# Attention scores by symmetry: score tiles left of the diagonal are fetched as transposes of tiles already computed

## The chip, the cores and the metric
The kernel runs on one core of one Trainium2 chip. The metric is the device time of one execution in microseconds, the median over several; the profile is of a single execution of its own. TensorE (PE) multiplies, VectorE (DVE) and ScalarE (ACT) work element by element, and the queue of SyncE (SP) issues all DMAs. All data is fp32; TensorE reads it in the form fp32r.

## The reference
```python
B, S, D = u.shape                                  # 2, 3008, 256; z has 64 columns
scores = (1.0 / S) * np.matmul(z, z.transpose(0, 2, 1))
attn = np.maximum(scores, 0.0) ** 2
x = (u * np.matmul(attn, v)).reshape(B * S, D)     # 6016 tokens
h = x @ w1_in;  x = (h - np.tanh(h)) @ w1_out      # d_ff 2048; the weights come in float64
h = x @ w2_in;  out = (np.maximum(h, 0) + alpha * np.minimum(h, 0)) @ w2_out
```
The scores are z times z transposed: the score of query s and key t is that of query t and key s, within one of the two sequences (batches).

## The kernel before
Every operand of a product is split into a high part (rounded to fp32r) and a low part (what is left), and a product is the sum of two or three matmuls: high by high, low by high, high by low. High parts are copies (L121), on ScalarE or VectorE; low parts are subtractions on VectorE (L124).

The work is cut into blocks of 512 tokens: a sequence of 3008 tokens has six, the last of 448. In the attention a block of queries i (q = 0 to 5 within its sequence) goes over 24 key tiles k of 128 keys; the last has 64 keys, doubled. One step is one key tile of one block. Its front (`front_products`, L296) is two matmuls with the keys as weights (L309): 128 keys by 512 queries of scores in PSUM. ScalarE applies relu and scale (L339), then the square (L342); the result `a` is split, the copy being on VectorE for the first block and for even k, on ScalarE otherwise (L345). The back (`back`, L381) is six matmuls (L396): two halves of v's 256 columns, three products each, added up in PSUM over the 24 steps; the last key tile has four. At a block's end `evacuate` multiplies by u on VectorE (L409) and stores x to DRAM (L410). The two MLPs have 16 steps a block, six front and six back matmuls a step, and more work on ScalarE and VectorE.

The order is written out by hand (`manual_schedule`). `steps` is one list: the attention's 288 steps, of which the last 24 take turns with steps of the first MLP, then both MLPs in turns. At turn t the loop (L504) issues the front of step t + 5 and the back of step t on TensorE; then the pieces deferred by earlier turns (`defer`, L291) and one piece of each load under way (`run_work`, L470); then `evacuate`, the DMAs of weights, and the first activation of step t + 5. What a part defers to turn r is issued r + 1 loops later, by rank. So the high and low parts of a step are issued two to four loops ahead of its back.

SBUF tiles are slots of 128 by 512 taken and dropped by hand from a first-in first-out list (`Slots`, L90): 84 of fp32r operands, 15 of raw data. Loads of z (L140) and v (L202) are asked for some steps ahead; queries are split by `load_queries` (L164), the first block by `load_first` (L169). Weights come in float64 and are taken apart into two fp32 parts by a chain of seven pieces (`split_f64`, L219: five two-source and two one-source instructions on VectorE, two on ScalarE), one piece a step and one weight tile every 7 steps, 16 for each MLP; those of the second are parked in DRAM and fetched again later (L500). The two series start at steps 20 and 142 (L457).

Of the kernel before, what the change touches and what calls it, by code (L numbers as in the profile page):

```python
# [17 lines left out]
P = 128  # L18
# [4 lines left out]
N_SLOTS = 84  # L23
# [14 lines left out]
def attention_two_mlps_kernel(  # L38
# [25 lines left out]

    nc = tc.nc
# [23 lines left out]

    class Slots:  # L90
# [20 lines left out]
    take, at, drop = mm.take, mm.at, mm.drop  # L111

# [3 lines left out]
    def split(h_key, l_key, src, n, on_vector=False, then=None):  # L116


        def high():
            copy = nc.vector.tensor_copy if on_vector else nc.scalar.copy  # L120
            copy(out=take(h_key)[:, :n], in_=src)  # L121

        def low():
            nc.vector.tensor_sub(out=take(l_key)[:, :n], in0=src, in1=f32(at(h_key)[:, :n]))  # L124
            if then:
                then()

        return [high, low]

# [34 lines left out]
    def load_queries(b, c):  # L164
        key = "zhh", b, c
        st, n = load_zt(key, b, c)
        return split(key, ("zll", b, c), st[:, :n], n, then=lambda: raw.drop(("st",) + key))

    def load_first():  # L169

        hl, hh, ll = ((z, 0, 0) for z in ("zhl", "zhh", "zll"))
        st, n = load_zt(hl, 0, 0)

        def low(c0, c1):
            nc.vector.tensor_sub(out=at(hl)[DQK:, c0:c1], in0=st[DQK:, c0:c1], in1=f32(at(hh)[DQK:, c0:c1]))  # L175

        def do():
            nc.vector.tensor_copy(out=take(hh), in_=st)  # L178
            nc.scalar.copy(out=take(hl)[:DQK], in_=st[:DQK])  # L179
            low(0, P)  # L180
            nc.vector.tensor_sub(out=take(ll), in0=st, in1=f32(at(hh)))
            low(P, n)
            raw.drop(("st",) + hl)

        return [do]
# [100 lines left out]

    banks = {}
    accs = {}
    turns = deque([] for _ in range(4))
# [6 lines left out]
    def front_products(kind, i, k):  # L296
        n = blocks[i][2]
# [24 lines left out]
    def front_activation(kind, i, k):  # L322

        n = blocks[i][2]
        ps = banks.pop((kind, i, k))
        key = kind, i, k

# [9 lines left out]
        if kind == 0:  # L337
# [42 lines left out]

    def back(kind, i, k):  # L381
# [4 lines left out]
        last = k == (KF if kind else KT) - 1  # L386
        if k == 0:
            accs[kind] = acc_pairs.popleft()
        acc = accs[kind]
        todo = [(wh, h), (wl, h), (wh, l)]  # L390
        if kind == 0 and last:
            todo = [(wh, h), (wh, l)]
        for d in range(KD):
            for e, (w, x) in enumerate(todo):
                c0 = o * D + d * P
                nc.tensor.matmul(out=acc[d][:, :n], lhsT=at(w)[:, c0:c0 + P], rhs=at(x)[:, :n],  # L396
                                 start=k == 0 and e == 0, stop=last and e == len(todo) - 1)
# [28 lines left out]
    streams = [[(0, i, k) for i in range(NBLK) for k in range(KT)]]  # L426
# [30 lines left out]
    for m, w_in, w_out, s0 in ((2, w2_in, w2_out, 20), (1, w1_in, w1_out, 142)):  # L457
# [43 lines left out]

    with tc.manual_schedule():
        warm_up()
        for t in range(-2 * LOOKAHEAD - LEAD, len(steps)):  # L504
# [17 lines left out]
            if t >= 0 and kind == 0 and k == KT // 2:  # L522
                load_u(i)
# [36 lines left out]
```

## Time and profile before
| | us |
|---|---|
| median of 3 runs (1548.41 to 1548.7) | 1548.49 |
| profiled execution, its time | 1548.68 |
| its span, first to last instruction | 1546.7 |
| busy: TensorE, ScalarE, VectorE | 1541.4, 1311.8, 1258.0 |
| TensorE on L396 and L309, modelled | 1002.0, 752.6 |
| DMA moved | 71.67 MB |

The attention takes the span up to about 567 us, its last 24 steps together with the first steps of the first MLP; the rest are the MLPs. Busy time of TensorE is modelled and pipelined: two matmuls overlap, so single durations (0.385 us) are longer than the pitch at which they follow each other. The granted clock is 1.00 over the span but for its first microseconds.

### The profile page before, as it was taken

Reading aid. Unit: us, or ns where it says so; the run is one execution under the profiler, and the core shown is the slowest. Engines: PE = TensorE matmul, PEld = TensorE weight load, DVE = VectorE, ACT = ScalarE, POOL = GpSimd, SP = SyncE. Lnnn points to the kernel's source line nnn. Section 1 sums busy time; section 2 is a strip of 40 time slices with the busy share of each in tenths; the row PEclk is TensorE's granted clock in tenths of the full one; section 3 lists DMA queues with packets and bytes.
Section 4 is the critical chain, followed back from the end, with each engine's and each line's share of the span. In section 5 each row is a group of like instructions: output and inputs, shape, how many; then the busy total and the mean of one; then the engine's idle time right before and its main releaser. Section 6 shows DMA issues by size and latency. Waiting matters only on the chain.

```text
span 1546.7 us, 19804 instructions
## 1 busy us (share of the span) xinstructions
PE 1541.4 (100%) x6895; PEld 1295.1 (84%) x6895; DVE 1258.0 (81%) x2164; ACT 1311.8 (85%) x2431; POOL 0.2 (0%) x4
## 2 busy tenths in 40 slices
PE   9999999999999999999999999999999999999999
PEld 7888889888888888888888888888888888888888
DVE  8888897777877898888787888888887888888764
ACT  8889998888888998888887888888888878888865
POOL 0000000000000000000000000000000000000000
PEclk9999999999999999999999999999999999999999
DMA  6234442122212230000000000000000000000000
GB/s 170 89 124 136 156 157 91 61 78 75 76 61 84 74 114 26 1 28 1 26 1 5 23 1 28 1 28 1 26 1 28 1 1 26 1 14 1 14 1 26
DMA packets 40660, 71.67 MB, mean 46 GB/s; under 512 B 6128, under 2 KB 14832, under 8 KB 40560
## 3 DMA queue, kind: packets, MB, share of 16 engines
q1 hardware_dynamic: 40560, 70.41, 14.2%
q8 instruction: 54, 0.88, 0.2%
q14 instruction: 46, 0.38, 0.1%
HBM read 49.68 MB, written 20.71 MB: 46 GB/s over the span
## 4 chain that ended last, share of the span: by engine, by line
PE 99%; DMA 0%; DVE 0%; SPq 0%; ACT 0%; issue 0%; DVEq 0%; ACTq 0%
PE acc L396 58%; PE front L309 42%; DMA raw<-in_zT 0%; SPq L140 0%; ACT raw L415 0%; DVE mm L178 0%; DVE mm L175 0%; DVEq L178 0%; ACTq L415 0%
## 5 line engine op out<-in xcount | busy, mean ns | idle before, releaser
L396 PE MATMUL acc<-mm,mm 128*128 128x512 f32 (+1 forms) x4008 | 1002.0, 385 | 0.0
L396 PEld LDWEIGHTS acc<-mm,mm 128*128 128x128 f32 x4008 | 752.6, 188 | 141.2
L309 PE MATMUL front<-mm,mm 128*128 128x512 f32 (+1 forms) x2880 | 752.6, 386 | 0.4 <-DVE mm L175 0.4
L309 PEld LDWEIGHTS front<-mm,mm 128*128 128x128 f32 x2880 | 541.6, 188 | 103.8 <-ACT mm L179 1.3
L124 DVE TENSOR_TENSOR mm<-raw,mm 128x512 fp32r<-128x512 f32 (+1 forms) x731 | 468.7, 676 | 3.7 <-PE acc L396 0.5
L121 DVE CAST mm<-raw 128x512 fp32r<-128x512 f32 (+1 forms) x360 | 151.6, 421 | 94.7 <-ACT raw L342 76.0
L121 ACT CAST mm<-raw 128x512 fp32r<-128x512 f32 (+1 forms) x371 | 223.2, 602 | 0.3 <-DVE raw L374 0.3
L360 DVE TENSOR_TENSOR raw<-front,raw 128x512 f32<-128x512 f32 (+1 forms) x192 | 130.5, 679 | 113.6 <-ACT raw L354 112.9
L350 ACT ACTIVATE raw<-front 128x512 f32<-128x512 f32 (+1 forms) x192 | 113.7, 592 | 121.0 <-PE front L309 120.9
L339 ACT ACTIVATE raw<-front 128x512 f32<-128x512 f32 (+1 forms) x288 | 168.9, 586 | 44.8 <-PE front L309 41.0
L342 ACT ACTIVATE raw<-raw 128x512 f32<-128x512 f32 (+1 forms) x288 | 179.8, 624 | 5.3
L374 DVE SCALAR_TENSOR_TENSOR raw<-raw,nalpha,raw 128x512 f32<-128x512 f32 (+1 forms) x192 | 141.4, 737 | 36.3 <-ACT raw L371 36.1
L363 DVE COPY_PREDICATED raw<-raw,raw 128x512 f32<-128x512 int32 (+1 forms) x192 | 142.9, 744 | 5.7
L357 DVE TENSOR_TENSOR raw<-front,raw 128x512 f32<-128x512 f32 (+1 forms) x192 | 129.7, 675 | 17.5 <-ACT raw L351 17.4
L370 ACT ACTIVATE raw<-front 128x512 f32<-128x512 f32 (+1 forms) x192 | 112.1, 584 | 19.4 <-PE front L309 18.2
L353 ACT ACTIVATE raw<-raw 128x512 f32<-128x512 f32 (+1 forms) x192 | 120.2, 626 | 6.1
L354 ACT ACTIVATE raw<-raw 128x512 f32<-128x512 f32 (+1 forms) x192 | 120.1, 626 | 6.1
L352 ACT ACTIVATE raw<-raw 128x512 f32<-128x512 f32 (+1 forms) x192 | 120.5, 628 | 0.0
L351 ACT ACTIVATE raw<-front 128x512 f32<-128x512 f32 (+1 forms) x192 | 112.9, 588 | 0.0
L371 ACT ACTIVATE raw<-front 128x512 f32<-128x512 f32 (+1 forms) x192 | 111.7, 582 | 0.0
L415 ACT COPY raw<-acc 128x512 f32<-128x512 f32 (+1 forms) x48 | 27.7, 580 | 27.2 <-PE acc L396 25.3
L238 DVE SCALAR_TENSOR_TENSOR raw<-st,raw 128x512 uint32<-128x512 uint32 x32 | 22.1, 690 | 2.1 <-ACT raw L232 1.0
(29 smaller groups left out, 222.5 us busy)
## 6 DMA issues: line engine op xcount, KB each, us to landing
st<-in_moe_w_in SPq DMA_DIRECT2D x16, 512.0 KB, 4.5
st<-in_moe_w_out SPq DMA_DIRECT2D x16, 512.0 KB, 3.8
raw<-in_v SPq DMA_DIRECT2D x22, 256.0 KB, 4.1
raw<-in_uT SPq DMA_DIRECT2D x20, 256.0 KB, 3.1
xd<-raw SPq DMA_DIRECT2D x20, 256.0 KB, 2.3
st<-xd SPq DMA_DIRECT2D x10, 512.0 KB, 3.7
outT<-raw SPq DMA_DIRECT2D x20, 256.0 KB, 2.0
raw<-in_zT SPq DMA_DIRECT2D x38, 128.0 KB, 4.0
```

The lines of the kernel that those rows point to most:

```text
L121: copy(out=take(h_key)[:, :n], in_=src)
L124: nc.vector.tensor_sub(out=take(l_key)[:, :n], in0=src, in1=f32(at(h_key)[:, :n]))
L309: nc.tensor.matmul(out=ps, lhsT=at(w)[:, o:o + P], rhs=at(x)[:, :n], start=e == 0, stop=e == len(todo) - 1)
L339: nc.scalar.activation(out=r, in_=ps, func=AF.Relu, scale=scale)
L342: nc.scalar.activation(out=a, in_=r, func=AF.Square)
L352: nc.scalar.activation(out=g, in_=g, func=AF.Arctan, scale=SMALL_C)
L353: nc.scalar.activation(out=g, in_=g, func=AF.Square, scale=SMALL_A)
L357: nc.vector.tensor_sub(out=t, in0=ps, in1=t)
L360: nc.vector.tensor_mul(out=g, in0=ps, in1=g)
L363: nc.vector.copy_predicated(out=t, mask=mask.bitcast(I32), data=g)
L374: nc.vector.scalar_tensor_tensor(out=r, in0=q, scalar=nalpha_sb[:, k:k + 1], in1=r, op0=ALU.mult, op1=ALU.add)
L396: nc.tensor.matmul(out=acc[d][:, :n], lhsT=at(w)[:, c0:c0 + P], rhs=at(x)[:, :n], start=k == 0 and e == 0, stop=last and e == len(todo) - 1)
```

## The change
In a block q of queries, the score tiles whose keys lie in a block kb < q (4q of 24) are no longer computed. They are the transposes of tiles of the earlier block kb of the same sequence, whose keys lay in block q. There, the squared tile `a` goes through one VectorE instruction that transposes it in 32 by 32 blocks into one of two buffers of four tiles; when the four tiles of a key block are there, SP writes them to DRAM in four DMAs, one for each 32 partitions, in rows of 128 elements (512 bytes). 12 steps ahead of its use SP loads the tile from DRAM into a slot; ScalarE copies the high part, and VectorE subtracts in place.

So that the 32 by 32 blocks come to lie right, the queries of a block stand in another column order (`in_columns`; `in_tokens` is the old one): the copies of the query loads, the multiplication by u and the first load use both views. The order of key tiles in a block changes for q > 0: first those of later blocks, then its own, evenly mixed with the fetched ones. High parts of tiles that are sent on are on ScalarE except every second in a block q = 0; those on the diagonal are on VectorE. The operand slots are 76 instead of 84 up to the attention's last block, when the two buffers are given back as 8 slots; keys and v are dropped as they are used up. The weight series start at steps 30 and 156.
```diff
-N_SLOTS = 84
+Q = 32
+FLIP_BUFS = 2
+FLIP_LEAD = 12
+N_SLOTS = 76
...
+    flip_pool = ExitStack()
+    flip_p = flip_pool.enter_context(tc.tile_pool(name="flip", bufs=1))
+    flip_bufs = [flip_p.tile([P, 4 * NB], F32, name=f"flip{i}") for i in range(FLIP_BUFS)]
...
+    def runs(n):
+
+        t = NB // P
+        if n == NB:
+            return [(0, 0, P // Q, t)]
+        half = HALF // Q
+        return [(0, 0, half, t), (half * t * Q, half, P // Q - half, t - 1)]
+
+    def in_columns(ap, n):
+
+        return [ap[:, c:c + na * nt * Q].rearrange("p (a t r) -> p t a r", a=na, t=nt) for c, _, na, nt in runs(n)]
+
+    def in_tokens(ap, n):
+
+        whole = ap.rearrange("p (t a r) -> p t a r", a=P // Q, r=Q)
+        return [whole[:, :nt, a:a + na] for _, a, na, nt in runs(n)]
...
+
+        def high():
+            for dst, src in zip(in_columns(take(key), n), in_tokens(st, n)):
+                nc.scalar.copy(out=dst, in_=src)
+
+        def low():
+            for dst, src, h in zip(in_columns(take(("zll", b, c)), n), in_tokens(st, n), in_columns(at(key), n)):
+                nc.vector.tensor_sub(out=dst, in0=src, in1=f32(h))
+            raw.drop(("st",) + key)
+
+        return [high, low]
...
         def do():
-            nc.vector.tensor_copy(out=take(hh), in_=st)
+            nc.vector.tensor_copy(out=in_columns(take(hh), n)[0], in_=in_tokens(st, n)[0])
             nc.scalar.copy(out=take(hl)[:DQK], in_=st[:DQK])
-            low(0, P)
-            nc.vector.tensor_sub(out=take(ll), in0=st, in1=f32(at(hh)))
-            low(P, n)
+            low(0, 1)
+            nc.vector.tensor_sub(out=in_columns(take(ll), n)[0], in0=in_tokens(st, n)[0],
+                                 in1=f32(in_columns(at(hh), n)[0]))
+            low(1, NB // P)
...
+    def key_tiles(q):
+
+        c = NB // P
+        if q == 0:
+            return list(range(KT))
+        mine = [k for kb in [*range(q + 1, QB), q] for k in range(kb * c, kb * c + c)]
+        theirs = list(range(q * c))
+        places = [((e + 0.5) / len(ks), k) for ks in (mine, theirs) for e, k in enumerate(ks)]
+        return [k for _, k in sorted(places)]
+
+    tiles_of = [key_tiles(q) for q in range(QB)]
+
+    def is_flipped(i, k):
+        return k * P // NB < i % QB
...
+        if kind == 0 and is_flipped(i, k):
+            return
...
-            if k == KT - 1:
+            if k == [k for k in tiles_of[q] if not is_flipped(i, k)][-1]:
                 drop(("zhh", b, q), ("zll", b, q))
-                if q == QB - 1:
-                    drop(*(("zhl", b, c) for c in range(QB)))
+                if q:
+                    drop(("zhl", b, q))
+                if q == 1:
+                    drop(("zhl", b, 0))
...
-        ps = banks.pop((kind, i, k))
         key = kind, i, k
+        if kind == 0 and is_flipped(i, k):
+            h, l = ("h",) + key, ("l",) + key
+
+            def high():
+                nc.scalar.copy(out=take(h)[:, :n], in_=f32(at(l)[:, :n]))
+
+            def low():
+                nc.vector.tensor_sub(out=at(l)[:, :n], in0=f32(at(l)[:, :n]), in1=f32(at(h)[:, :n]))
+
+            defer((0, 0, high), (1, 3, low))
+            return
+        ps = banks.pop(key)
...
-            on_vector = i == 0 or k % 2 == 0
-            high, low = parts(a, "a", on_vector)
+            b, q = blocks[i][0], i % QB
+            kb, t = divmod(k, NB // P)
+            flip = kb > q
+            on_vector = not flip or q == 0 and k % 2 == 0
+            high, low = split(("h",) + key, ("l",) + key, a, n, on_vector, then=None if flip else lambda: free("a"))
             defer((0, 0, square), (1, 0, high), (1 if on_vector else 2, 3, low))
+
+            def transpose():
+                if t == 0:
+                    flip_bufs.append(flip_bufs.pop(0))
+                buf = flip_bufs[-1]
+                nc.vector.transpose(out=buf.rearrange("p (t a s r) -> p a t s r", t=NB // P, a=P // Q, r=Q)[:, :, :, t],
+                                    in_=a.rearrange("p (a t r) -> p a t r", a=P // Q, r=Q))
+                free("a")
+                if t < NB // P - 1:
+                    return
+                m = blocks[b * QB + kb][2]
+                flips[b, q, kb] = to = dram.tile([NB, m], F32, name=f"flip_{b}_{q}_{kb}")
+                for c, a0, na, nt in runs(m):
+                    for e in range(na):
+                        p0 = (a0 + e) * Q
+                        nc.sync.dma_start(
+                            out=to.rearrange("(f r) c -> r f c", r=Q)[:, :, c + e * nt * Q:c + (e + 1) * nt * Q],
+                            in_=buf[p0:p0 + Q].rearrange("p (f c) -> p f c", c=P)[:, :, :nt * Q])
+
+            if flip:
...
+    def ends(kind, i, k):
+
+        ks = range(KF) if kind else tiles_of[i % QB]
+        return k == ks[0], k == ks[-1]
...
+        first, last = ends(kind, i, k)
+        if first:
             accs[kind] = acc_pairs.popleft()
         acc = accs[kind]
         todo = [(wh, h), (wl, h), (wh, l)]
-        if kind == 0 and last:
+        if kind == 0 and k == KT - 1:
...
-        if k % 2 and i == (NBLK if kind else QB * (b + 1)) - 1:
-            drop(wh, wl)
+        if i == (NBLK if kind else QB * (b + 1)) - 1:
+            used.add((kind, b, k))
+            if (kind, b, k ^ 1) in used:
+                drop(wh, wl)
...
-                x = raw.at(("u", i, d))[:, :n]
-                nc.vector.tensor_mul(out=x, in0=acc[d][:, :n], in1=x)
-                nc.sync.dma_start(out=x_dram[i][:, d, :n], in_=x)
+                x = raw.at(("u", i, d))
+                for there, here in zip(in_columns(acc[d], n), in_tokens(x, n)):
+                    nc.vector.tensor_mul(out=here, in0=there, in1=here)
+                nc.sync.dma_start(out=x_dram[i][:, d, :n], in_=x[:, :n])
...
-    streams = [[(0, i, k) for i in range(NBLK) for k in range(KT)]]
+    streams = [[(0, i, k) for i in range(NBLK) for k in tiles_of[i % QB]]]
...
-    for m, w_in, w_out, s0 in ((2, w2_in, w2_out, 20), (1, w1_in, w1_out, 142)):
+    for m, w_in, w_out, s0 in ((2, w2_in, w2_out, 30), (1, w1_in, w1_out, 156)):
...
+    flipped = deque((t, *step[1:]) for t, step in enumerate(steps) if step[0] == 0 and is_flipped(*step[1:]))
+
+    def run_flipped(t):
+        while flipped and flipped[0][0] <= t + FLIP_LEAD:
+            _, i, k = flipped.popleft()
+            b, _, n = blocks[i]
+            kb, e = divmod(k, NB // P)
+            nc.sync.dma_start(out=f32(take(("l", 0, i, k))[:, :n]), in_=flips[b, kb, i % QB][e * P:(e + 1) * P])
...
-            if t >= 0 and k == (KF if kind else KT) - 1:
+            if t >= 0 and ends(kind, i, k)[1]:
                 evacuate(kind, i)
+            if t == n_att - KF * 3 // 2:
+                flip_pool.close()
+                more = ctx.enter_context(tc.tile_pool(name="more", bufs=1))
+                mm.free.extend(range(N_SLOTS, N_SLOTS + 4 * FLIP_BUFS))
+                mm.tiles += [more.tile([P, NB], F32R, name=f"mm{N_SLOTS + e}") for e in range(4 * FLIP_BUFS)]
+            run_flipped(t)
...
-            if t >= 0 and kind == 0 and k == KT // 2:
+            if t >= 0 and kind == 0 and k == tiles_of[i % QB][KT // 2]:
```

## Rows read from the trace of the kernel before
**Rows 1.** The page's head: span, busy time, granted clock in 40 slices.
```profile
span 1546.7 us, 19804 instructions
PE 1541.4 (100%) x6895; PEld 1295.1 (84%) x6895; DVE 1258.0 (81%) x2164; ACT 1311.8 (85%) x2431; POOL 0.2 (0%) x4
...
PEclk9999999999999999999999999999999999999999
```
**Rows 2.** The chain of waits that ended last, on the page, by line.
```profile
PE acc L396 58%; PE front L309 42%; DMA raw<-in_zT 0%; SPq L140 0%; ACT raw L415 0%; DVE mm L178 0%; DVE mm L175 0%; DVEq L178 0%; ACTq L415 0%
```
**Rows 3.** List of waits: us in total, times, longest.
```profile
DVE mm L121 <- ACT raw L342: 76.0, 88, 1.9
```
**Rows 4.** Timeline of TensorE: start, us, engine, line, operation.
```profile
441.55 0.62 PE L309 MATMUL front<-mm,mm 128*128 128x512 f32 x2
442.00 1.52 PE L396 MATMUL acc<-mm,mm 128*128 128x512 f32 x6
```
**Rows 5.** Timeline of SP's queue: three of the stores of x.
```profile
225.50 1.30 SPq L410 DMA_DIRECT2D xd<-raw  x2
...
264.26 0.87 SPq L410 DMA_DIRECT2D xd<-raw  x2
...
307.38 0.92 SPq L410 DMA_DIRECT2D xd<-raw  x2
```
**Rows 6.** Windows, one per block: engines' busy us (instructions), clock, DMA share, GB/s.
```profile
10.00:53.00 43.00, 43.00 (x191) 35.37 (x190) 39.37 (x75) 39.84 (x73) 0.00 (x0) 1.00 0.40 107
53.00:96.00 43.00, 43.00 (x191) 35.61 (x190) 34.51 (x65) 37.90 (x69) 0.00 (x0) 1.00 0.34 116
96.00:139.00 43.00, 43.00 (x191) 35.64 (x190) 35.35 (x66) 38.50 (x71) 0.00 (x0) 1.00 0.45 141
139.00:182.00 43.00, 43.00 (x192) 35.61 (x191) 37.03 (x68) 39.31 (x73) 0.00 (x0) 1.00 0.42 135
182.00:225.00 43.00, 43.00 (x192) 35.78 (x191) 38.89 (x72) 41.13 (x78) 0.00 (x0) 1.00 0.58 177
225.00:264.00 39.00, 39.00 (x192) 35.87 (x192) 30.28 (x60) 35.43 (x71) 0.00 (x0) 1.00 0.28 93
264.00:307.00 43.00, 43.00 (x191) 35.58 (x191) 34.40 (x64) 38.05 (x69) 0.00 (x0) 1.00 0.21 66
307.00:350.00 43.00, 43.00 (x192) 35.61 (x191) 34.34 (x64) 37.60 (x68) 0.00 (x0) 1.00 0.26 80
...
436.00:479.00 43.00, 43.00 (x192) 35.67 (x191) 30.28 (x56) 36.55 (x68) 0.00 (x0) 1.00 0.16 54
479.00:567.00 88.00, 88.00 (x405) 75.73 (x404) 79.83 (x139) 83.72 (x157) 0.00 (x0) 1.00 0.29 90
```
**Rows 7.** Timeline of VectorE, where it is saturated.
```profile
22.54 0.42 DVE L121 CAST mm<-raw 128x512 fp32r<-128x512 f32 x1
22.99 0.69 DVE L124 TENSOR_TENSOR mm<-raw,mm 128x512 fp32r<-128x512 f32 x1
23.60 0.42 DVE L121 CAST mm<-raw 128x512 fp32r<-128x512 f32 x1
23.95 1.30 DVE L124 TENSOR_TENSOR mm<-raw,mm 128x512 fp32r<-128x512 f32 x2
25.16 0.42 DVE L121 CAST mm<-raw 128x512 fp32r<-128x512 f32 x1
```
**Rows 8.** VectorE's groups: busy us, mean ns; the second from 53 to 479 us.
```profile
L363 DVE COPY_PREDICATED raw<-raw,raw 128x512 f32<-128x512 int32 (+1 forms) x192 | 142.9, 744 | 5.7
...
L234 DVE TENSOR_SCALAR raw<-st 128x512 uint32<-128x512 uint32 x31 | 13.1, 422 | 0.0
```
**Rows 9.** DMA: packets by size, the queue, and x's store with its landing.
```profile
DMA packets 40660, 71.67 MB, mean 46 GB/s; under 512 B 6128, under 2 KB 14832, under 8 KB 40560
...
q1 hardware_dynamic: 40560, 70.41, 14.2%
...
xd<-raw SPq DMA_DIRECT2D x20, 256.0 KB, 2.3
```

More of the change, by code (lines that the diff above doesn't have):

```diff
@@ L166, in load_queries @@
         st, n = load_zt(key, b, c)
-        return split(key, ("zll", b, c), st[:, :n], n, then=lambda: raw.drop(("st",) + key))
+        def high():
[6 more added lines that the diff above has]
+        return [high, low]
     def load_first():
@@ L172, in load_first, with low @@
         st, n = load_zt(hl, 0, 0)
-        def low(c0, c1):
-            nc.vector.tensor_sub(out=at(hl)[DQK:, c0:c1], in0=st[DQK:, c0:c1], in1=f32(at(hh)[DQK:, c0:c1]))
+        def low(t0, t1):
+            nc.vector.tensor_sub(out=in_tokens(at(hl), n)[0][DQK:, t0:t1], in0=in_tokens(st, n)[0][DQK:, t0:t1],
+                                 in1=f32(in_columns(at(hh), n)[0][DQK:, t0:t1]))
         def do():
-            nc.vector.tensor_copy(out=take(hh), in_=st)
+            nc.vector.tensor_copy(out=in_columns(take(hh), n)[0], in_=in_tokens(st, n)[0])
             nc.scalar.copy(out=take(hl)[:DQK], in_=st[:DQK])
-            low(0, P)
-            nc.vector.tensor_sub(out=take(ll), in0=st, in1=f32(at(hh)))
-            low(P, n)
+            low(0, 1)
+            nc.vector.tensor_sub(out=in_columns(take(ll), n)[0], in0=in_tokens(st, n)[0],
+                                 in1=f32(in_columns(at(hh), n)[0]))
+            low(1, NB // P)
             raw.drop(("st",) + hl)
@@ L285, in load_x @@
                 for piece in split(("xh", 1, i, d), ("xl", 1, i, d), st[:, d, :n], n, on_vector=d == 1)]
+    def key_tiles(q):
[9 more added lines that the diff above has]
+        return k * P // NB < i % QB
     banks = {}
     accs = {}
+    flips = {}
+    used = set()
     turns = deque([] for _ in range(4))
@@ L343, in square @@
                 free("r")
-            on_vector = i == 0 or k % 2 == 0
-            high, low = parts(a, "a", on_vector)
-            defer((0, 0, square), (1, 0, high), (1 if on_vector else 2, 3, low))
+            b, q = blocks[i][0], i % QB
[3 more added lines that the diff above has]
+            high, low = split(("h",) + key, ("l",) + key, a, n, on_vector, then=None if flip else lambda: free("a"))
+            defer((0, 0, square), (1, 0, high), (1 if on_vector else 2, 3, low))
+            def transpose():
[16 more added lines that the diff above has]
+            if flip:
+                defer((2, 4, transpose))
         elif kind == 1:
@@ L385, in back @@
         wh, wl = (("vh", b, j), ("vl", b, j)) if kind == 0 else (("woh", kind, j), ("wol", kind, j))
-        last = k == (KF if kind else KT) - 1
-        if k == 0:
+        first, last = ends(kind, i, k)
+        if first:
             accs[kind] = acc_pairs.popleft()
@@ L396, in back @@
                 nc.tensor.matmul(out=acc[d][:, :n], lhsT=at(w)[:, c0:c0 + P], rhs=at(x)[:, :n],
-                                 start=k == 0 and e == 0, stop=last and e == len(todo) - 1)
+                                 start=first and e == 0, stop=last and e == len(todo) - 1)
         drop(h, l)
-        if k % 2 and i == (NBLK if kind else QB * (b + 1)) - 1:
-            drop(wh, wl)
+        if i == (NBLK if kind else QB * (b + 1)) - 1:
+            used.add((kind, b, k))
+            if (kind, b, k ^ 1) in used:
+                drop(wh, wl)
     def evacuate(kind, i):
```

## Prediction
> **What bounds the kernel now.** I read the page's head first. [...] A busy TensorE alone proves nothing, since matmuls are pipelined, so the chain of waits came next: 99% of it are the two matmul lines, L396 and L309, and no other engine holds it for as much as 0.5% [rows 2]. The list of waits has the same answer from the other side: the engines wait for each other, VectorE's casts 76.0 us for ScalarE's square [rows 3], while TensorE waits for nobody after the first microseconds. So a matmul that goes is worth its whole pitch, as long as the other engines follow.
>
> What a matmul costs in the attention stage: an L309 pair starts at 441.55 and the six of L396 behind it at 442.00 [rows 4], so two matmuls take 0.45 us. More exactly from whole blocks: the issues of x's store come 43.12 us apart for a block of 512 queries and 38.76 us for one of 448 [rows 5]. A block has 24 x 8 - 2 = 190 matmuls, which gives 0.2269 and 0.2040 us each.
>
> VectorE is the engine to watch. In a block of the attention it is busy 34.3 to 38.9 of 43 us, ScalarE 36.6 to 41.1 [rows 6]. ScalarE is the busier one; the change relieves it and loads VectorE.
>
> **Removed matmuls.** A block q (0 to 5 in its batch) takes 4q of its 24 score tiles as transposes: 60 a batch, 120 in all. Each saves the two matmuls of L309. The 448-wide block q = 5 has 20 of the 60, so 80 tiles x 2 x 0.2269 = 36.3 us and 40 tiles x 2 x 0.2040 = 16.3 us: **52.6 us** off TensorE's path. The output products (L396) stay as many, and the two MLPs are untouched.
>
> **ScalarE.** 120 tiles lose relu and square and gain one copy (their high part), and in the sending tiles the high part moves to ScalarE. Fewer instructions in every block but the first of each batch, where up to 10 casts are added to an engine that was busy 39.8 of 43 us with more loads around it [rows 6]. No cost.
>
> **VectorE.** Its price of an instruction is not its duration but its pitch when it is saturated, and the stretch from 22 to 25 us shows that: a two-source subtraction of 0.69 us is followed after 0.61 us, two of them after 1.21; a cast (0.42 us) after 0.35, or after 0.45 where its own subtraction waits for it [rows 7].
> The transpose is nowhere in this trace. Bounds: below, the pitch of a one-source SBUF-to-SBUF instruction at VectorE's double pace, 0.34 (a duration of 0.42 less the overlap of 0.08; 0.422 in [rows 8]); above, 0.75, the slowest 512-wide instruction (0.744 us) with no overlap at all [rows 8]. Its output does not stand in the order of its input, which no double-pace row here has, so I take it nearer to the two-source instructions, 0.61 and a little for the strided output: 0.64.
> [...]
>
> Now block by block, VectorE's busy time of [rows 6] with three corrections: casts that go or move (before, all 24 tiles of the first block and 12 of every other; after, 14 in a block q = 0 and 4 in the others, so -8 x 0.45 = -3.6 us in most), transposes (20, 16, 12, 8, 4, 0 by block, at 0.64), and the weight staging, which starts later (steps 30 and 156 instead of 20 and 142). Staging is five instructions at 0.61 and two at 0.34 for every 7 steps, 0.53 us a step [rows 7, 8]. Against it stands the block's time on TensorE, 43.1 us less 0.454 us for each tile saved (0.408 at 448).
> Batch 0: q0 39.4 - 2.1 - 4.6 + 12.8 = 45.5 against 43 (over by 2.5); q1 34.5 - 3.6 + 10.2 - 3.2 = 37.9 against 41.3; q2 35.4 - 3.6 + 7.7 = 39.5 against 39.5; q3 37.0 - 3.6 + 5.1 = 38.5 against 37.7 (over 0.8); q4 38.9 - 3.6 + 2.6 = 37.9 against 35.8 (over 2.1); q5 30.3 - 3.4 + 5.3 = 32.2 against 30.6 (over 1.6).
> Batch 1: q0 34.4 + 0.9 + 12.8 - 6.4 = 41.7 against 43.1; q1 34.3 - 3.6 + 10.2 = 40.9 against 41.3; q2 and q3, from windows within 0.1 us of that, 38.5 and 35.9 against 39.5 and 37.7; q4 30.3 - 3.6 + 2.6 + 5.3 = 34.6 against 35.8; the last block with the MLP's first steps 79.8 - 3.2 + 2.1 = 78.7 against 79.8.
> So VectorE needs 92 to 106% of the shortened blocks. The overs add up to **7.0 us**. Some of that is absorbed: at 22 to 25 us VectorE is saturated [rows 7] while TensorE is busy without a gap [rows 6], since a tile is prepared two to five steps before it is used. But an engine near 100% also loses time to waits that the sums don't show. I let the two cancel and charge 7.0; the ends are 0 (transposes at 0.34 take 36 us off VectorE, and only the last two blocks of batch 0 are over, by 2.5 us together, which the lead can absorb) and about 22 (at 0.75, 120 x 0.11 = 13 us more, nearly all of it in blocks that are full, and 2 of waits).
>
> **DMA and SP.** Each group of four transposed tiles (1.05 MB, 30 groups) is written by four DMAs in pieces of 512 B, 2048 a group, and 120 loads of 224 or 256 KB bring the tiles back. SP issues two DMAs in 0.92 us [rows 5]: 240 more cost about 110 us of a queue that has some 440. What waits behind them on SP are loads and stores with 8 to 14 steps of lead. A tile is fetched 12 steps ahead, at least 16 us; 256 KB land in 2.3 us [rows 9]. Its group was written in an earlier block of the same batch. Hidden.
> A group's buffer is filled again after the next group: in a block q = 0 that leaves 5 steps, 9.1 us, for four writes, and one group each 8.6 us to sustain. If the write is later, the next transpose waits on VectorE with every subtraction behind it, and TensorE for those. The write's price per packet isn't in the trace. From below, by bytes: q1 moved 70.41 MB in 14.2% of 16 x 1546.7 us, 320 GB/s, so 3.3 us a group. From above, the mean packet at any size: 3514 us / 40560 = 87 ns, so 11.1 us a group [rows 9]. Few packets there are below 1 KB other than tiny ones, so neither end is shown; I take about 4 us, hidden, since the transfer by bytes lies nearer to rows of large tiles as these are.
>
> **The rest.** The first query load is copied in another order: 0 to 0.25 us on the start (a cast at 0.69 instead of 0.44); I take 0.2. The slots fall from 84 to 76 until the attention's last block. Their scarcity would show as ScalarE or VectorE waiting for L396, and a slot is written four steps before it is read; nothing is charged, up to 4 us is kept for the range.
>
> **Sum.** The profiled execution took 1548.7 us, 2.0 around its span of 1546.7; the median of the runs is 1548.5, so no correction. 1548.5 - 52.6 + 7.0 + 0.2 = **1503 us**.
>
> **Rivals.**
> *VectorE sets the pace* (1509 to 1530). For it: 92 to 106% leaves no room for a transpose at 0.75 or for one wait of 0.1 us a step. Against it: the waits of VectorE for ScalarE [rows 3] shrink with the casts. Price 22 us or more: about 1518.
> [...]
> *A packet costs the same at any size: slower.* Place: the transpose's wait for its buffer, in the blocks q0 to q2. A group of X us in a queue already taken by 40, 34 and 45% in batch 0 and 21 to 26% in batch 1 [rows 6] needs X/(1 - share), against 8.6, 10.3 and 13.1 us a group. The excess eats the 52.6 us at X near 8.2, 64 ns a packet, which lies between the ends. At X = 9 it loses 76 us: about 1573. Against it: 512 B would then move at 8 GB/s per engine where the mean is 20. [...]
> That the change doesn't remove what it says can be left out: the skipped tiles issue no L309 matmul.
>
> **Chances.** Forecast (1496 to 1508) 0.54; VectorE's pace 0.23; half paths 0.11; packets 0.08 slower; between the last two, no change, 0.04. Faster 0.88, same (within 0.2%, 3 us, what a measurement can tell) 0.04, slower 0.08. The range 1494 to 1528 holds the forecast, most of VectorE's pace and of the half paths; about 0.18 is outside.
>
> **What would show it.** L309 falls from 2880 to 2640 matmuls. Right: block periods from 43 down to about 36 us in batch 0, TensorE's idle below 8 us, the chain still above 97% TensorE, the transpose's mean near 0.7 us. Wrong: L396 waiting for VectorE's subtractions for over 15 us (pace), the transposes waiting for DMA (buffers), or L396 waiting for ScalarE's copies of fetched tiles (the round trip). [...]

## The result: 1510.1 us, and the profile after

| | before | after |
|---|---|---|
| median, us (4 runs each, side by side) | 1548.45 (1548.37 to 1548.7) | 1510.13 (1509.3 to 1512.08) |
| span of the profiled execution | 1546.7 | 1508.5 |
| busy: TensorE, ScalarE, VectorE | 1541.4, 1311.8, 1258.0 | 1494.3, 1231.0, 1288.7 |
| DMA moved, MB | 71.67 | 131.97 |

The ratio is 0.9754, 95% interval 0.9737 to 0.9771. The kernel is faster by 38.3 us, 7 less than forecast: of the 52.6 us of matmuls removed, 14.4 came back as something else (by spans, 1546.7 - 52.6 = 1494.1 against 1508.5).

The chain of waits of the kernel after, by engine and by line, answers to [rows 2]:
```profile
PE 92%; DMA 4%; DVE 2%; ACT 1%; SPq 1%; issue 1%; DVEq 0%; ACTq 0%
```
TensorE holds 92% of it, not 99%: DMA, VectorE, ScalarE and SP now hold some stretches. The list of waits (who waits for whom: us in total, times, longest) has TensorE and the two new lines in it, and below it stands what SP's queue waits for at the writes:
```profile
PEld acc L499 <- DVE mm L137: 8.4, 10, 3.0
ACT mm L393 <- DMA mm<-flip: 6.7, 5, 2.0
PE acc L499 <- DVE mm L137: 4.3, 5, 2.6
DVE flip L430 <- DMA flip<-flip: 2.2, 2, 2.0
...
SPq L440 <- DVE flip L430: 73.1, 22, 8.6
```
No wait is large by itself. TensorE waits for VectorE's subtractions (L137), ScalarE for fetched tiles (L393), VectorE once for a buffer (L430), and SP stands 73 us at the writes (L440) until the transposes are done.

The windows of the six blocks of batch 0 answer to the first six of [rows 6] (busy us of TensorE, its weight loads, VectorE, ScalarE, GpSimd; granted clock; DMA share; GB/s):
```profile
10.00:57.50 47.50, 44.90 (x186) 35.37 (x185) 44.39 (x80) 42.36 (x81) 0.00 (x0) 0.96 0.71 193
57.50:97.80 40.30, 40.30 (x179) 33.36 (x179) 36.02 (x65) 36.22 (x67) 0.00 (x0) 1.00 0.82 236
97.80:138.10 40.30, 40.30 (x180) 33.36 (x179) 39.48 (x70) 35.26 (x63) 0.00 (x0) 1.00 0.91 279
138.10:176.70 38.60, 38.60 (x172) 31.97 (x171) 37.45 (x68) 31.43 (x56) 0.00 (x0) 1.00 0.92 296
176.70:218.00 41.30, 39.60 (x172) 31.15 (x170) 40.84 (x74) 28.27 (x54) 0.00 (x0) 1.00 0.98 314
218.00:249.00 31.00, 29.40 (x136) 24.91 (x137) 29.30 (x57) 20.69 (x41) 0.00 (x0) 1.00 0.74 248
```
VectorE is busy for 89 to 99% of each, and DMA, which was at 28 to 58%, is at 71 to 98%. A modelled TensorE without a gap in the second to fourth windows does not say by itself that it lost nothing there: it is pipelined (0.386 us a matmul, where the next follows after 0.227), and the length of the block has to be looked at.

The loss is placed by the blocks' ends on TensorE: the start of the last of a block's matmuls at L499 (before: L396), read from the trace. The end without loss is that of before less 0.454 us (0.408 at 448) for each saved tile whose front would have been issued up to there (before: 52.71, 263.61 and 585.18 us). The first block's end lies in these four matmuls, before and after:
```profile
52.03 1.07 PE L396 MATMUL acc<-mm,mm 128*128 128x512 f32 x4
```
```profile
56.87 1.08 PE L499 MATMUL acc<-mm,mm 128*128 128x512 f32 x4
```

| end of | without loss, us | after | lost since the row above |
|---|---|---|---|
| the first block | 52.26 | 57.56 | 5.3 |
| batch 0 | 237.29 | 249.39 | 6.8 |
| batch 1 | 532.54 | 547.03 | 2.4 |

The MLPs lose nothing. Block by block the loss is all in a few places: 5.3 in the first block, 2.0 and 4.7 in the last two of batch 0, 2.4 where batch 1 ends beside the first MLP. The second to fourth blocks take 40.80, 38.99 and 37.63 us, which is 43.07 less 5, 9 and 12 tiles at 0.454: they lose nothing, with VectorE busy for 89 to 98% and DMA for 82 to 92%. VectorE's multiplication by u does not mark the end as well: it comes 0.3 us later in the kernel after, and up to 3 us later in kernels below, where VectorE lags and TensorE does not wait for it. The rest of this text uses the same three sums for other kernels: "loses a + b + c".

The first block has the one large stall. VectorE's timeline (start, us; in brackets the idle time ahead and who ended it), then TensorE's, then windows of the stall (columns as above):
```profile
46.37 0.70 DVE L430 STREAM_TRANSPOSE flip<-raw 128x512 f32<-128x512 f32 x1
49.10 0.71 DVE L430 STREAM_TRANSPOSE flip<-raw 128x512 f32<-128x512 f32 x1 [2.03 <-DMA flip<-flip]
```
```profile
47.39 1.98 PE L499 MATMUL acc<-mm,mm 128*128 128x512 f32 x8
51.96 1.96 PE L499 MATMUL acc<-mm,mm 128*128 128x512 f32 x4 [2.59 <-DVE mm L137]
```
```profile
46.00:49.50 3.50, 3.37 (x15) 2.48 (x14) 1.47 (x3) 3.47 (x8) 0.00 (x0) 1.00 1.00 267
49.50:51.90 2.40, 0.00 (x0) 0.00 (x0) 2.33 (x6) 1.60 (x3) 0.00 (x0) 1.00 0.92 268
51.90:55.40 3.50, 3.44 (x8) 2.70 (x9) 3.50 (x7) 0.60 (x1) 0.00 (x0) 0.53 0.99 307
```
A transpose waits 2.03 us for its buffer, all subtractions stand behind it, TensorE idles 2.59 us, and then its granted clock is lower for some 3.4 us (0.53 in the third window, 0.50 in each microsecond from 53 to 55), which do the work of 1.7. So this wait cost about 4.3 of the block's 5.3 us in this execution.

Why the buffer is late shows in SP's queue at 24 to 46 us (start, duration of the issues, line); the buffer is the one whose write was issued from 40.09 on and landed at 48.91:
```profile
24.77 3.07 SPq L440 DMA_DIRECT2D flip<-flip  x4
27.94 2.12 SPq L244 DMA_DIRECT2D raw<-in_v  x2
...
32.27 3.29 SPq L440 DMA_DIRECT2D flip<-flip  x4
...
40.09 5.35 SPq L440 DMA_DIRECT2D flip<-flip  x4
45.48 1.18 SPq L615 DMA_DIRECT2D mm<-flip  x1
```
Four writes are issued in 3.1 to 5.4 us where two stores of x took 0.92 [rows 5], and loads of v stand behind a write that waits: the pair issued at 27.94 was issued at 17.68 before.

### The profile page after: what moved, and what is told of

It is laid out like the page before. It is cut to its first block, busy times and chain, and to the rows that moved or that the text cites. A ratio compares the mean times of both kernels' runs of the same rounds, so it can differ in the third digit from the quotient of the medians.

```text
span 1508.5 us, 19589 instructions
## 1 busy us (share of the span) xinstructions
PE 1494.3 (99%) x6655; PEld 1248.2 (83%) x6655; DVE 1288.7 (85%) x2202; ACT 1231.0 (82%) x2281; POOL 0.2 (0%) x4
## 2 busy tenths in 40 slices
DMA packets 121301, 131.97 MB, mean 87 GB/s; under 512 B 20208, under 2 KB 85232, under 8 KB 121200
## 3 DMA queue, kind: packets, MB, share of 16 engines
q1 hardware_dynamic: 121200, 130.72, 28.2%
## 4 chain that ended last, share of the span: by engine, by line
PE 92%; DMA 4%; DVE 2%; ACT 1%; SPq 1%; issue 1%; DVEq 0%; ACTq 0%
PE acc L499 54%; PE front L370 38%; DMA mm<-flip 1%; DVE mm L137 1%; DMA raw<-in_v 1%; DMA raw<-in_zT 1%; DMA st<-in_moe_w_out 0%; SPq L440 0%; ACT raw L413 0%; DMA w_woh<-mm 0%; DMA w_wil<-mm 0%; DVE mm L396 0%; DVE flip L430 0%; ACT raw L416 0%; SPq L615 0%
## 5 line engine op out<-in xcount | busy, mean ns | idle before, releaser
L499 PE MATMUL acc<-mm,mm 128*128 128x512 f32 (+1 forms) x4008 | 988.9, 386 | 7.5 <-DVE mm L137 4.3
L499 PEld LDWEIGHTS acc<-mm,mm 128*128 128x128 f32 x4008 | 751.6, 188 | 156.5 <-DVE mm L137 8.4
L370 PE MATMUL front<-mm,mm 128*128 128x512 f32 (+1 forms) x2640 | 679.6, 386 | 1.8 <-DVE mm L188 0.9
L370 PEld LDWEIGHTS front<-mm,mm 128*128 128x128 f32 x2640 | 495.6, 188 | 97.2 <-DVE mm L188 1.6
L137 DVE TENSOR_TENSOR mm<-raw,mm 128x512 fp32r<-128x512 f32 (+1 forms) x600 | 389.7, 675 | 4.3 <-ACT mm L134 1.7
L448 ACT ACTIVATE raw<-front 128x512 f32<-128x512 f32 (+1 forms) x192 | 113.4, 591 | 128.7 <-PE front L370 128.6
L134 ACT CAST mm<-raw 128x512 fp32r<-128x512 f32 (+1 forms) x328 | 198.4, 606 | 1.3 <-DVE raw L472 0.3
L413 ACT ACTIVATE raw<-front 128x512 f32<-128x512 f32 (+1 forms) x168 | 99.4, 592 | 45.4 <-PE front L370 44.2
L134 DVE CAST mm<-raw 128x512 fp32r<-128x512 f32 (+1 forms) x272 | 113.6, 418 | 25.6 <-ACT raw L416 7.0
L468 ACT ACTIVATE raw<-front 128x512 f32<-128x512 f32 (+1 forms) x192 | 112.1, 584 | 19.4 <-PE front L370 18.3
L452 ACT ACTIVATE raw<-raw 128x512 f32<-128x512 f32 (+1 forms) x192 | 119.8, 624 | 6.1
L451 ACT ACTIVATE raw<-raw 128x512 f32<-128x512 f32 (+1 forms) x192 | 119.7, 623 | 6.1
L450 ACT ACTIVATE raw<-raw 128x512 f32<-128x512 f32 (+1 forms) x192 | 120.3, 627 | 0.0
L449 ACT ACTIVATE raw<-front 128x512 f32<-128x512 f32 (+1 forms) x192 | 112.8, 588 | 0.0
L469 ACT ACTIVATE raw<-front 128x512 f32<-128x512 f32 (+1 forms) x192 | 111.5, 581 | 0.0
L416 ACT ACTIVATE raw<-raw 128x512 f32<-128x512 f32 (+1 forms) x168 | 106.1, 632 | 3.5
L430 DVE STREAM_TRANSPOSE flip<-raw 128x512 f32<-128x512 f32 x120 | 83.3, 700 | 2.2 <-DMA flip<-flip 2.2
L393 ACT CAST mm<-mm 128x512 fp32r<-128x512 f32 (+1 forms) x120 | 70.4, 595 | 12.5 <-DMA mm<-flip 6.7
```

What stands on the lines that cost most here:

```text
L370: nc.tensor.matmul(out=ps, lhsT=at(w)[:, o:o + P], rhs=at(x)[:, :n], start=e == 0, stop=e == len(todo) - 1)
L448: nc.scalar.activation(out=g, in_=ps, func=AF.Tanh, scale=SMALL_B)
L450: nc.scalar.activation(out=g, in_=g, func=AF.Arctan, scale=SMALL_C)
L451: nc.scalar.activation(out=g, in_=g, func=AF.Square, scale=SMALL_A)
L452: nc.scalar.activation(out=mask, in_=g, func=AF.Relu, scale=-1.0, bias=SMALL_F)
```

## Experiments

All were timed in three rounds. The first four ran beside each other, as did the next four, the next three, and the last by itself; before took 1548.8 to 1549.0 beside them. Two theories for the 14.4 us: VectorE has no room (pace), or the writes and fetches come late (DMA and SP's queue).

**small_writes.** Each write is cut to a sixteenth, and all fetches read one fixed tile; VectorE has all its work.
```diff
-out=to.rearrange("(f r) c -> r f c", r=Q)[:, :, c + e * nt * Q:c + (e + 1) * nt * Q],
+out=to.rearrange("(f r) c -> r f c", r=Q)[:, :1, c + e * nt * Q:c + (e + 1) * nt * Q],
...
-in_=flips[b, kb, i % QB][e * P:(e + 1) * P])
+in_=other[:, :n])
```


> Of each group of transposed tiles only a sixteenth is written (rows of one 128-row tile), and the fetched tiles come from one fixed DRAM tile instead, so that no fetch waits for a write; what is added up is then not the reference's. VectorE and ScalarE do all they did. Theory P (VectorE's work exceeds the shortened blocks): only the 2.0 us of waiting for a buffer in the first block and some of the stall behind it go, 1505 to 1508 us. Rival W (the write, its buffer and the round trip): most of the 14 us go, 1500 us or less.


Measured 1504.6 us (1504.54 to 1504.97), ratio 0.9715 (0.9701 to 0.973). The fixed tile's own load stands at the head of the queue, and the first back matmul starts at 12.30 us, where it was 10.12 before; less these 2.2 us it is 1502.4. That is under P's range and above W's. It loses 3.1 (2.2 of it the start) + 3.8 + 2.4. So 7.7 of the 14.4 us need the transfers, and some 7 do not. VectorE is as full as in the changed kernel, in the fourth block of it 37.93 of 38 us, and TensorE has no gap:
```profile
137.00:175.00 38.00, 38.00 (x170) 31.47 (x169) 37.93 (x69) 31.50 (x56) 0.00 (x0) 1.00 0.78 256
```

**short_transpose.** A transpose takes 128 of the 512 columns; all transfers stay. What is sent on is mostly zeros.
```diff
-nc.vector.transpose(out=buf.rearrange("p (t a s r) -> p a t s r", t=NB // P, a=P // Q, r=Q)[:, :, :, t],
+nc.vector.transpose(out=buf.rearrange("p (t a s r) -> p a t s r", t=NB // P, a=P // Q, r=Q)[:, :1, :, t],
```


> Each transpose handles 128 of its 512 columns (the rest of the buffer is zero), so that a transpose should cost VectorE some 0.2 us instead of 0.62, 48 us less in all; writes, buffers and fetches are as they were. P: the loss nearly goes, 1497 to 1501 us. W: 1506 or more.


Measured 1503.43 us (1503.22 to 1504.13), ratio 0.9708 (0.9694 to 0.9723): between the two. A transpose takes 0.30 us now. It loses 1.6 + 3.5 + 2.4. Room on VectorE alone recovers 6.7 us, with all of the DMA traffic in place.

**no_staging.** The chain that takes the float64 weights apart is left out on VectorE, two copies on ScalarE stay; the weights are not the right ones. That chain starts in the second block, so the first block's instructions are those of the changed kernel.
```diff
-        return [fields, mantissa, sign, high, low, rest, finish]
+        return [nothing, nothing, nothing, nothing, low, nothing, finish]
```


> The weights' high and low parts are both plain copies on ScalarE of one half of the float64 words, so the seven VectorE instructions of each of the 32 weight tiles (3.7 us each, 120 us) are left out, and so is the right value of the weights. Weight DMAs stay. P: what was lost from block 2 to the end of the first sequence goes (about 7 us), the first block's 5 to 7 us stay: 1501 to 1504. W: 1508 to 1510.


Measured 1500.96 us (1500.43 to 1503.05), ratio 0.9694 (0.968 to 0.9708): at the low end of what the pace theory had. It loses 3.0 + 1.6 + 0.0: behind the first block next to nothing. The first block, with the same instructions, loses 2.3 us less than in the changed kernel's profile: its longest idle time on TensorE is 1.74 us, not 2.59, and its granted clock stays at 1.00. TensorE's end of the block, then VectorE's multiplication, 2.5 us behind it:
```profile
54.57 1.07 PE L478 MATMUL acc<-mm,mm 128*128 128x512 f32 x4
```
```profile
57.72 1.25 DVE L494 TENSOR_TENSOR raw<-acc,raw 128x512 f32<-128x512 f32 x2
```
Two windows of batch 0:
```profile
137.00:175.00 38.00, 38.00 (x170) 31.46 (x169) 26.59 (x45) 31.51 (x56) 0.00 (x0) 1.00 1.00 314
175.00:213.00 38.00, 38.00 (x172) 31.98 (x171) 27.48 (x47) 28.50 (x54) 0.00 (x0) 1.00 1.01 314
```
DMA is fully taken (1.00), at least as much as in the changed kernel, and TensorE loses nothing in these two blocks (the changed kernel: 2.0 us in the second of them) once VectorE has 28 to 30% to spare. A busy DMA is no cost of its own here.

**diag_on_act.** The high parts of the diagonal tiles go from VectorE to ScalarE, which has room (67 to 90% busy).
```diff
-on_vector = not flip or q == 0 and k % 2 == 0
+on_vector = q == 0 and (not flip or k % 2 == 0)
```


> In blocks q > 0 the four casts of the tiles on the diagonal go from VectorE (0.35 to 0.45 us each) to ScalarE, which was busy 21 to 36 of 31 to 41 us there: 1.6 us a block, 16 us of VectorE's work. P: 3 to 5 us faster than the changed kernel, 1505 to 1507. W: no change, 1510.


Measured 1513.52 us (1513.02 to 1514.03), ratio 0.9771 (0.9755 to 0.9788): the expectation of a gain failed; by the medians it is 3.4 us slower than the changed kernel, though the ratios' intervals overlap. It loses 4.8 + 11.3 + 2.1; the last block of batch 0 shows a lower granted clock and TensorE's gaps:
```profile
218.40:254.00 35.60, 31.37 (x136) 27.25 (x135) 28.10 (x53) 22.46 (x43) 0.00 (x0) 0.90 0.67 219
```
In ScalarE's program these casts now stand behind its copies of fetched tiles. That this is the cause was not tested.

**lead16 and lead8.** A tile is fetched 16 or 8 steps ahead instead of 12.
```diff
-FLIP_LEAD = 12
+FLIP_LEAD = 16
```


> Transposed tiles are fetched 16 steps ahead instead of 12. After the first four runs the theory is J: the loss is joint, VectorE has no room left and fetched tiles and freed buffers come late, because in the first sequence the DMA engines are taken to 82 to 98%. J: fewer late fetches, 1506 to 1509 us. Rival P (VectorE's work alone): no change, 1509 to 1511.


Measured 1512.64 us (1512.03 to 1513.05), ratio 0.9767 (0.9752 to 0.9781): failed, and outside the rival's range too. ScalarE no longer waits for fetched tiles, but 6.9 + 8.1 + 2.1 are lost, with a granted clock of 0.93 in the first block. An earlier fetch takes its slot earlier, and stands ahead of loads on SP; that this is the cause was not tested.


> Fetched 8 steps ahead instead of 12; also the control for the next kernel. J: more fetches late, 1514 us or more. P: no change.


Measured 1532.47 us (1532.24 to 1533.38), ratio 0.9896 (0.9881 to 0.9911): held. It loses 2.7 + 30.1 + 3.9. The wait that was 6.7 us has become
```profile
ACT mm L393 <- DMA mm<-flip: 85.9, 39, 6.9
```
though the fetches land in 5.1 us (median) and 8 steps are some 10 us or more. What eats the lead lies before the issue: SP reaches a fetch late, behind writes that wait for transposes (79.7 us here) and fetches that wait for a slot (31.5). Lead in the program's order is not lead in time.

**three_bufs_lead8.** A third buffer at the cost of four slots, with the lead of 8 to make room: to be read against lead8.
```diff
-FLIP_BUFS = 2
-FLIP_LEAD = 12
-N_SLOTS = 76
+FLIP_BUFS = 3
+FLIP_LEAD = 8
+N_SLOTS = 72
```


> Three buffers for the transposed tiles instead of two (72 slots, fetched 8 steps ahead to make room). If the first block's loss comes of the 2.0 us wait for a buffer and the lower clock behind it, this is 4 to 5 us faster than the same with two buffers; if it is VectorE's work in that block, the two are equal.


Measured 1531.48 us (1529.27 to 1532.71), ratio 0.9887 (0.9872 to 0.9902). VectorE never waits for a buffer, and the time is that of lead8 within their intervals. It loses 1.3 + 28.2 + 3.9: the first block, with a clock of 1.00 in both, loses 1.4 us less than in lead8. At this lead, which has a bound of its own, the third buffer is worth about 1 us, not 4 to 5; at the lead of 12 it was not tried.

**gp_writes.** GpSimd, idle so far, issues the writes; SP keeps the rest.
```diff
-                        nc.sync.dma_start(
+                        nc.gpsimd.dma_start(
                             out=to.rearrange("(f r) c -> r f c", r=Q)...
```


> The four writes of each group are issued from GpSimd, which is idle otherwise, so that loads and fetches on SP no longer stand behind writes that wait for a transpose (9.1 us in the first 58). If that waiting matters: 1505 to 1508 us. [...]


Measured 1506.4 us (1505.42 to 1508.3), ratio 0.973 (0.9714 to 0.9747): held. Against the changed kernel the ratios' intervals still touch, the runs themselves do not (1509.3 at the least there). It loses 3.0 + 4.7 + 2.1: against the changed kernel 2.3 us less in the first block, where the granted clock stays at 1.00, and 2.1 less in the rest of batch 0. The wait for the transposes has moved with the issue (busy us, mean ns, idle before):
```profile
L440 POOL DMA_DIRECT2D flip<-flip x120 | 80.3, 676 | 339.8 <-DVE flip L430 332.7
```

**later_writes.** The same cure without GpSimd: SP issues a group's writes two loops later, behind the loads and fetches of those loops.
```diff
+                def write():
                     for c, a0, na, nt in runs(m):
...
+                defer((1, 5, write))
```


> The four writes of a group are issued on SP as before, but two loops later than the group's last transpose, behind the loads and fetches of those loops; nothing else changes, GpSimd issues nothing. Q (what gp_writes took off, 3.7 us, was that loads and fetches stood on SP's queue behind writes whose transposes were not done): the same gain without GpSimd, 1505 to 1508, and SP waits at L440 for VectorE for under 35 us instead of 73. G (the gain came from GpSimd's queue itself, which moves the same bytes in fewer records, 9280 instead of some 63,000): 1509 to 1511. B (in block 0 the two buffers come free still later when the writes start later, and TensorE stands for it): above 1511.


Measured 1506.43 us (1505.47 to 1506.86), ratio 0.9723 (0.9707 to 0.9739): the order on SP's queue is enough for the gain, without the other queue. It loses 2.1 + 6.8 + 2.1. In this profile nearly all of the gain is in the first block, where VectorE's wait for a buffer is 0.2 us and the clock stays at 1.00; what gp_writes took off the rest of batch 0 is not there, and whether its queue or chance did that is open, with one profile of each. The wait at the writes came out longer than expected (under 35):
```profile
SPq L442 <- DVE flip L430: 47.7, 17, 6.9
```
gp_writes and later_writes are the two fastest kernels that compute everything.

**gp_short.** Both remedies: writes from GpSimd, short transposes.


> The writes are issued by GpSimd as in gp_writes (1506.4), and each transpose takes 128 of its 512 columns as in short_transpose (1503.4); what is sent on is mostly zeros, the transfers stay. V+Q (VectorE without room and the writes that wait on SP's queue are two causes, each with its own price): the gains of the two add up, 3.7 and 6.7 us off 1510.1, so 1499.7 (1498.5 to 1501), block 0 ends near 55.8 us. One cause (both remedies only remove the same few stalls): no better than the better of the two, 1502.5 to 1504.


Measured 1505.54 us (1504.67 to 1506.35), ratio 0.972 (0.9705 to 0.9734): neither. The two gains do not add up; together they are no better than gp_writes, and 2 us behind short_transpose. It loses 4.6 + 3.3 + 2.1. VectorE's waits for buffers are up, where they were 2.2 us after the change, 5.1 in gp_writes and 4.6 in short_transpose:
```profile
DVE flip L433 <- DMA flip<-flip: 7.8, 6, 3.3
```
GpSimd's writes land in 5.3 us (median), SP's in 4.2 in short_transpose. Against short_transpose the 3.0 us are lost in the first block: 1.0 before its first back matmul, the rest where VectorE waits for buffers (5.4 us in that block) and the clock falls (0.96). A VectorE with room runs up against the buffers, and these come free later. That reading of the trace was not tested by itself.

**gp_low0 and gp_pool_low.** Real room for VectorE: as gp_writes, with subtractions moved to GpSimd; five in the first block of each batch, or the 120 of the fetched tiles.
```diff
+            if flip and q == 0 and k % 4 == 1:
+                def low():
+                    nc.gpsimd.tensor_sub(out=take(("l",) + key)[:, :n], in0=a, in1=f32(at(("h",) + key)[:, :n]))
```
```diff
-nc.vector.tensor_sub(out=at(l)[:, :n], in0=f32(at(l)[:, :n]), in1=f32(at(h)[:, :n]))
+nc.gpsimd.tensor_sub(out=at(l)[:, :n], in0=f32(at(l)[:, :n]), in1=f32(at(h)[:, :n]))
```


> As gp_writes, and in the first block of each batch the low part of 5 of the 24 tiles is subtracted on GpSimd, which has only the writes to issue. V (block 0's loss of 5.9 us in gp_writes is VectorE's lack of room: 45.5 us busy of 48.8): 5 x 0.61 = 3 us off VectorE, block 0 ends at 56 to 57.5 instead of 58.8, time 1503.5 to 1505. D (block 0 is late through buffers and DMA): 1506 to 1507. G (GpSimd's subtraction, not in any trace yet, is so slow that TensorE waits for it, or its queue's waits for transposes hold it up): above 1507.

> As gp_writes, and all 120 subtractions in place of fetched tiles are on GpSimd: VectorE loses 120 x 0.61 = 73 us of the attention, none of it in the first blocks. V: the rest of batch 0 loses 1.8 us in gp_writes and batch 1 2.4; with room on VectorE both go to about 0, as in no_staging: 1502 to 1504. G (GpSimd takes over 1.5 us for one, or holds VectorE up while both read SBUF, or its queue's waits hold the subtractions up beyond the four steps of lead): TensorE waits for GpSimd, 1508 or more.


Measured 1513.24 us (1512.02 to 1515.42), ratio 0.9771 (0.9756 to 0.9786), and 1556.84 us (1555.13 to 1558.19), ratio 1.0052 (1.0036 to 1.0069): in both GpSimd's rival held, and the second eats the whole gain. In gp_low0 TensorE waits for the subtractions on GpSimd themselves:
```profile
PE acc L503 <- POOL mm L426: 7.2, 5, 1.9
```
It loses 7.4 + 5.2 + 4.2; against gp_writes the first block of batch 0 loses 4.4 us more and that of batch 1 2.2, the two that hold these subtractions. gp_pool_low loses 3.9 + 31.7 + 24.4, and TensorE waits for VectorE more than for GpSimd:
```profile
PE acc L499 <- DVE mm L137: 18.6, 18, 2.1
PE acc L499 <- POOL mm L396: 9.4, 7, 2.5
```
The reason for the first of these is in VectorE's busy time. It should have fallen by 79.2 us and rose from 1288.7 (1289.0 in gp_writes) to 1338.9. GpSimd's timeline, then VectorE's, of the same microseconds:
```profile
99.88 1.70 POOL L396 TENSOR_TENSOR mm<-mm,mm 128x512 fp32r<-128x512 f32 x1 [6.42 <-ACT mm L393]
...
109.56 2.55 POOL L396 TENSOR_TENSOR mm<-mm,mm 128x512 fp32r<-128x512 f32 x2
```
```profile
100.34 1.78 DVE L137 TENSOR_TENSOR mm<-raw,mm 128x512 fp32r<-128x512 f32 x1
102.04 0.70 DVE L430 STREAM_TRANSPOSE flip<-raw 128x512 f32<-128x512 f32 x1
...
108.81 3.85 DVE L284 TENSOR_TENSOR raw<-raw,raw 128x512 uint32<-128x512 uint32 x1
```
L137 and L284, 0.6 to 0.7 us by themselves, last until GpSimd's subtractions are over and some 0.55 us more (102.12 against 101.58, 112.66 against 112.11).

## Why the prediction was right in kind and 7 us off

**Removed matmuls: right.** L370 has 2640 matmuls:
```profile
L370 PE MATMUL front<-mm,mm 128*128 128x512 f32 (+1 forms) x2640 | 679.6, 386 | 1.8 <-DVE mm L188 0.9
```
The second to fourth blocks, which are shorter by 0.454 us for each saved tile to within 0.02 us, show that they are worth their pitch.

**The transpose: right.** Predicted 0.64 us of pitch between 0.34 and 0.75; 120 of them took 0.70 each, and two that follow each other 1.30, so they overlap by 0.1 and the pitch is 0.60 to 0.63:
```profile
39.11 1.30 DVE L430 STREAM_TRANSPOSE flip<-raw 128x512 f32<-128x512 f32 x2
40.33 0.38 DVE L134 CAST mm<-raw 128x512 fp32r<-128x512 f32 x1
```
The cast behind the two starts at 40.33, 0.08 us before they end, as one does behind a subtraction in [rows 7]. What the working calls double pace is there a cast's pitch of 0.35 us beside a subtraction's 0.61; the transpose goes with the latter. VectorE's sum rose by 30.7 us, where the working above makes it some 37.

**Writes and fetches by bytes: right in price.** The writes have 512-byte pieces, and queue q1 now has
```profile
q1 hardware_dynamic: 121200, 130.72, 28.2%
```
Against [rows 9] that is 28.2% x 1508.5 - 14.2% x 1546.7 = 205.8 us of all 16 engines for 60.31 MB more, 293 GB/s where the queue had 320: a group with its fetches takes 6.9 us, about 3.7 of them the write if the fetches go at 320 (4 taken). The rival of a price by the packet had 8.2 or more: it is out, and with it the slower side. Half paths, with 0.11 among the chances, are shown by no run here; by the estimate above a group's write came to about 3.7 us.

**ScalarE, the start, the slots.** No cost on ScalarE to be seen, and none at the start (the first cast takes 0.43 us as before, and the first back matmul starts at 9.97 us, 10.12 before). The slots' scarcity does not show where I looked for it, but on SP: fetches wait 44.2 us for a slot that L499 still reads; what that costs was not tested.

**"Hidden" for DMA and SP: the step that failed.** I charged nothing. Three things were wrong in it.
- SP's queue was counted as 110 us of 440, by the sum. But SP issues in the program's order, and a write waits for a transpose: 73 us in 22 waits, with the loads, fetches and stores behind it. What counts is not the queue's sum but who stands behind its longest wait. Price by gp_writes and later_writes: 3.7 us; with small writes 7.7 go.
- An issue was taken at 0.46 us; a group's four writes take 3.1 to 5.4 us in the first block instead of 1.84.
- A write was set beside the DMA share of before alone. With its own fetches and the writes of others the share is 0.71 to 0.98, and loads that landed in 3.1 and 4.1 us (u, v) land in 5.2 and 4.8. So the buffer's 9.1 us, which I called enough, were short once by 2.03 us.

**VectorE's 7.0 us: right in kind, short in size.** "I let the two cancel" was the weak sentence: the steps of lead absorb lateness only if nothing else uses them up. By no_staging against the changed kernel the blocks behind the first lose 5.2 us in batch 0 and 2.4 in batch 1 to it, 4.5 and 0 were charged. The places are nearly those of the sums: over by 0.8, 2.1 and 1.6 us in q3, q4 and q5 of batch 0, lost 0, 2.0 and 4.7. The first block was charged 2.5 us and lost 5.3, of it 4.3 at the one wait for a buffer and after it the clock, which the sum did not have; where the clock did not fall, in no_staging, the same instructions lose 3.0. The time came out at the low end of the rival "VectorE sets the pace" (1509 to 1530), but VectorE's pace alone did not bring it there: SP's order was a part, with 3.7 us.

**The signs.** Of those named, the transpose's 0.70 us and the L370 count came as written; the chain's 92% (above 97% expected) and TensorE's idle time, 14.2 us (below 8 expected), said wrong. L499's waits for VectorE's subtractions, its weight loads' and its matmuls' together, are 17.0 us (12.7 for L137, 4.3 for the fetched tiles' L396), above the mark of 15; the matmuls' alone are 5.4. So the sign of VectorE's pace came, and weakly. The transposes' wait for DMA, the sign of the buffers, is 2.2 us in all, 2.0 of it in the first block. Slips in the working do not move the forecast: VectorE's 34.3 to 38.9 us leave out 39.4 and 30.3 in [rows 6], which the sums use; ten casts at 0.45 are 4.5 us, not 4.6; and 1548.5 - 52.6 + 76 is 1572, not 1573.

**How the causes go together.** The 9.2 us lost behind the first block fall to 1.6 if VectorE has room (no_staging, DMA just as full), and to 6.2, 6.8 and 8.9 if the writes are small, are issued elsewhere or later (VectorE as full). So there it is VectorE's work above all, and the transfers make it dearer: a late tile costs little where the engine that prepares it can catch up. A VectorE that is nearly full, but not over, costs nothing by itself, as the second to fourth blocks show. In the first block the transfers weigh more: of 5.3 us 0.9 are left with small writes (3.1 less the start), 2.1 with later writes, and 1.6 with short transposes. The gains of such remedies do not add up (gp_short).

A part of the first block's loss differs between executions of the same instructions, by whether the clock falls. Its granted clock was 0.93 to 0.96 in the profiles of the changed kernel, diag_on_act, gp_short and lead16, which lose 4.6 to 6.9 us there, and 1.00 in the others, which lose 1.3 to 3.9, but for gp_low0 with its waits for GpSimd. Over whole executions the changed kernel's clock was 0.999 in three of four, that of gp_writes and later_writes 1.000 in all. So some of their 3.7 us is the clock that did not fall; how much is open.

## What to carry to other kernels

Where an engine is brought to 89 to 99% of a block, ask whether its work fits block by block: three blocks at 89 to 98% lost nothing here, and most of the loss came where the sum was over. Then ask what can come late, as it has nothing left to catch up with. Of a DMA that waits for its data, list what stands behind it on the same queue; issue it later in the order, after what needs no wait, or from another queue. Here one line of order was worth 3.7 us, a tenth of what the whole change brought.

## Of the hardware, not expected

- GpSimd's subtraction (128x512, fp32) takes 1.38 us on average in gp_low0 and 1.44 in gp_pool_low (a third of them 448 wide), and there each cost VectorE (1338.9 - 1288.7 + 79.2) / 120 = 1.08 us. In batch 0, VectorE's groups of gp_pool_low (busy us, mean ns):
```profile
L137 DVE TENSOR_TENSOR mm<-raw,mm 128x512 fp32r<-128x512 f32 x79 | 65.7, 840 | 0.3
L430 DVE STREAM_TRANSPOSE flip<-raw 128x512 f32<-128x512 f32 x46 | 31.9, 699 | 1.4 <-DMA flip<-flip 1.4
L515 DVE TENSOR_TENSOR raw<-acc,raw 128x512 f32<-128x512 f32 x8 | 5.0, 667 | 0.0
```
  The subtraction from SBUF rose from 682 to 840 ns; the transpose and the multiplication with one source in PSUM, 702 and 672 after the change, did not. Not only two-source instructions were slowed: VectorE's casts of 128x512 from SBUF (L134) rose from 414 to 549 ns in the same stretch.
- In the profile of the changed kernel a single idle time of 2.59 us on TensorE was followed by 3.4 us at a granted clock of 0.50 to 0.53, a cost two thirds as large as the wait itself.
